# Retention and MLP interleaved on one core: one burst of small matmuls per chunk, and a reordered first batch

## The chip, the cores and the metric

The kernel runs on one core of a Trainium2 chip. The metric is the device time of one execution in microseconds (us), the median of several runs. Before the change it is 234.43 us (five runs, 233.9 to 240.18).

The engines are named as in the profile: PE is TensorE (the matrix array; PEld its weight loads), DVE is VectorE, ACT is ScalarE, POOL is GpSimd, SP is the sync engine, which here only issues DMAs. Each engine works through its own list of instructions in order.

## What is computed

Four batches, eight heads, 768 tokens, head size 64. A retention layer is followed by a low-rank token mixer and an MLP with a residual:

```python
for t in range(S):                       # per batch and head
    state = gamma * state + outer(k[t], v[t])
    y[t] = q[t] @ state / sqrt(D)
x = y, heads side by side                # [B, 768, 512]
h = x.transpose(0, 2, 1) @ U @ V         # low rank, over tokens; rank 32
u = x + h.transpose(0, 2, 1)
out = u + relu(u @ w_ch1) @ w_ch2        # 512 -> 2048 -> 512
```

Inputs and output are float32; the kernel computes its matmuls in bf16 and accumulates in float32 in PSUM.

## The kernel before

**Retention by chunks.** The recurrence is cut into chunks of 128 tokens, six per batch. For each chunk and head the kernel takes the *score* (k times q, masked to the causal half), the *mix* (masked score times v), the *query* (q times the state of the chunks before) and the *state* (k times v, added up in PSUM). The decay is put into q and v as factors when they are cast to bf16.

**Batches 1 to 3** are woven into the MLP of the batch before. `mlp_pieces` (L458) gives the MLP as a list of pieces with a cost: `up` pieces (L463: four matmuls and a relu, either 512 or 256 tokens wide, every third relu on DVE, the rest on ACT) and `down` pieces (L486: four matmuls; the last of a row adds the residual on DVE and queues a store). `weave` (L522) puts the pieces out in order and, at given fractions of their total cost (41.5 for a batch), calls the retention parts. The fractions are in `AT` and `LR` (L760 and L761), with one row for batch 1 and one for batches 2 and 3. For every chunk there are these calls:

- `turn_chunk` (L307): DVE turns k and q of the chunk, L313.
- `score4` (L356): sixteen matmuls on 32-row tiles of the array (L363), then two products with the mask on DVE (L369). In batches 2 and 3 the state follows at once (`state`, L332: sixteen matmuls on 32-column tiles, L348, and a copy on ACT to `ns`). In batch 1 k in natural order is first made with four matmuls (`natural_k`, L319).
- `mix4` (L377), a little later: sixteen query matmuls on 32-row tiles (L387; none for chunk 0), eight mix matmuls on the full array (L396), and two copies of x on ACT. In batch 1 the state comes behind it.
- `prep_chunk` (L266): POOL casts k, q and v of a later chunk (L83, L85). The order on POOL in batch 1 is k, q, v of chunk 0, then of chunk 1, and so on, with DMA issues for weights and for half of q between them.

Score and mix share the PSUM tiles `R[0]` and `R[1]`, two banks each. The tag `mlp` has three banks, used in turn by the MLP pieces and by `natural_k`. After the last chunk come `lr_proj` (L411), `lr_expand` (L421) and `lr_turn` (L436); in batches 2 and 3 the last is a DMA transpose issued by SP (L439).

**Batch 0** has no MLP to hide in and runs first, in 256-token blocks of its own layout, in an order written out by hand (L672 to L738): `cast_early`, `turn_early` (PE transposes and a copy), `score_early`, `state_early`, `query_early`, `mix_early`. At its end PE turns x (`x_turn`), forms the projection (`proj`, one copy `pc` on DVE), and adds the product with V (L732). The result is copied to `uT` in four pieces, two on ACT and two on DVE (L737). `late_consts` (L226) then makes the mask and the decay factors for the other batches: ten small DVE operations and two exponentials on ACT, and its second exponential needs the last of the DVE operations.

**DMA.** SP issues all input loads but those of the weights and part of batch 1's q, in program order with at most eight under way. Batch 1's v arrives by chunk at L133. POOL issues the weight loads (L291, L296), the rest of q and the stores (L456).

The order of each engine is the order of the program text as the weave calls it; tiles give the waits, and a PSUM bank that two engines use is handed from one to the other.

Of the kernel before, what the change touches and what calls it, by code (L numbers as in the profile page):

```python
# [10 lines left out]
bf16 = mybir.dt.bfloat16  # L11
# [5 lines left out]
def kernel(  # L17
# [12 lines left out]
    P = 128  # L30
# [39 lines left out]
    def evac(eng, dst, src):  # L70
        if eng == "A":
            nc.scalar.activation(dst, src, AF.Copy)  # L72
        else:
            nc.vector.tensor_copy(out=dst, in_=src)
# [241 lines left out]
    def turned(nm, b, ci, i, c, r=slice(None)):  # L316
        return bts[nm, b, ci][r, i, c]
# [12 lines left out]
        live["kn", b, ci] = kn  # L330

    def state(b, ci):  # L332
        if ci == NCK - 1:
            return
        vb = pre["v", b, ci]
        if b > 1:
            kd = pre.pop(("k", b, ci)).rearrange("p (n i) (c w) -> p i c n w",
                                                 i=2, c=2)
        else:
            kd = live.pop(("kn", b, ci))[:, :512].rearrange(  # L340
                "p (i c n w) -> p i c n w", i=2, c=2, n=4)
        if ci == 0:
            live["st_p", b] = bank("st")
        st_p = live["st_p", b]
        for i in range(2):
            for c in range(2):
                for hp in range(4):
                    nc.tensor.matmul(st_p[ds(32 * hp, 32), ts(2 * i + c, D)],  # L348
                                     kd[:, i, c, hp], vb[:, 2 * hp + i],
                                     start=(ci == 0 and i == 0 and c == 0),  # L350
                                     stop=True, skip_group_check=True)
        ns = rmid.tile([P, 320], bf16, tag="ns", name=f"ns_{b}_{ci}")
        evac("A", ns[:, :256], st_p[:, :256])
        live["state", b, ci] = ns

    def score4(b, ci):  # L356
        if b == 1:
            natural_k(b, ci)
        for i in range(2):
            for c in range(2):  # L360
                for hp in range(4):
                    r = ds(32 * hp, 32)
                    nc.tensor.matmul(R[hp // 2][:, hp % 2, ts(i, P)],  # L363
                                     turned("kT", b, ci, i, c, r),
                                     turned("qT", b, ci, i, c, r), start=(c == 0),
                                     stop=(c == 1))
        a = rmid.tile([P, H, P], bf16, tag="a4", name=f"a4_{b}_{ci}", bufs=3)
        for g in range(2):
            nc.vector.tensor_tensor(  # L369
                a[:, ds(4 * g, 4)].rearrange("p (n i) m -> p n i m", n=2),  # L370
                R[g][:, :, :256].rearrange("p n (i m) -> p n i m", i=2),
                mask[:, None, None, :].to_broadcast([P, 2, 2, P]), op=ALU.mult)
        live["a", b, ci] = a
        if b > 1:
            state(b, ci)

    def mix4(b, ci):  # L377
        if ci == 0 and b > 1:
            open_x(b)
        vb, a = pre["v", b, ci], live.pop(("a", b, ci))  # L380
        if ci:
            st = live.pop(("state", b, ci - 1))
            for i in range(2):
                for c in range(2):
                    for hp in range(4):
                        r = ds(32 * hp, 32)
                        nc.tensor.matmul(R[hp // 2][:, hp % 2, ts(i, D)],  # L387
                                         turned("qT", b, ci, i, c, r),
                                         st[r, ts(2 * i + c, D)],
                                         start=(i == 0 and c == 0), stop=False,  # L390
                                         skip_group_check=True)
        x4 = four(xs[b][:, ci])
        for g in range(2):
            for i in range(2):
                for hp in (2 * g, 2 * g + 1):
                    nc.tensor.matmul(R[g][:, hp % 2, ts(i, D)], a[:, 2 * hp + i],  # L396
                                     vb[:, 2 * hp + i],
                                     start=(ci == 0 and i == 0), stop=True,
                                     skip_group_check=True)
            evac("A", x4[:, ds(2 * g, 2)], R[g][:, :, :P])  # L400
        if b == 1:
            state(b, ci)
        pre.pop(("v", b, ci))

    us, uTs, pcs = {}, {}, {}

# [51 lines left out]
    def mlp_pieces(b):  # L458
# [17 lines left out]
            return f  # L476

        run = NM // 2 if b == 0 else NM
        for m0 in range(0, NM, run):
            for m in range(m0, m0 + run):  # L480
                pieces.append((0.864, up(m, 0, LO)))
            for m in range(m0, m0 + run):
                pieces.append((0.432, up(m, LO, S - LO)))
# [148 lines left out]
            if 2 * B0 + cc < LAST:  # L632
                query_early(2 * B0 + cc, o[cc])

    def mix_early(B0, engines="AA", open_mix=open_mix, late=None):
        if open_mix:
            open_mix(B0)
        o = mixing[B0]
        for g in range(2):
            a = eb["a", B0, g]  # L640
            for n in range(2):
                for i in range(2):
                    h = 4 * g + 2 * n + i
                    for j in range(2):
                        for cc in range(2):
                            r = ds(64 * cc, 64)
                            first = 2 * B0 + cc in (0, LAST) and h == 0 and j == 0
                            nc.tensor.matmul(
                                o[cc][:, ts(h, D)], a[r, 2 * i + n, ts(j, P)],
                                eb["v", B0][r, j, h], start=first, stop=True,  # L650
                                skip_group_check=True)
        if 2 * B0 + 1 == LAST:
            evac(engines[0], xs[0][:, 2 * B0], o[0])
            query_early(LAST, o[1])
            evac(engines[1], xs[0][:, LAST], o[1])
        else:
            evac(engines[0], xs[0][:, 2 * B0], o[0])
            if late:
                late(2 * B0 + 2)
            evac(engines[1], xs[0][:, 2 * B0 + 1], o[1])  # L660
        for key in (("a", B0, 0), ("a", B0, 1), ("qT", B0), ("v", B0), ("k", B0)):
            del eb[key]

# [18 lines left out]
    turn_early("k", 1)  # L682
    state_early(1)
    cast_early("q", 1, ("P", 4, 4), ("D", 0, 4))
    mix_early(0)
    turn_early("q", 1, "D")
    cast_early("v", 1, ("P", 0, 4), ("P", 4, 4))
    cast_early("q", 2, ("P", 4, 4), ("D", 0, 4))
    state_early(2)
# [3 lines left out]
    turn_early("q", 2)  # L693
    cast_early("k", 2, ("P", 0, 4), ("P", 4, 4))
    turn_early("k", 2, "D")
    cast_early("v", 2, ("P", 0, 4), ("P", 4, 4))
    load_uv()
    load_w1(1)
    cast_uv("u")
# [4 lines left out]
    cast_uv("v")  # L704
    open_mix(1)
    score_early(2)
    mix_early(1, "AD", open_mix=False, late=state_early)
    p_p = bank("mlp")

    def proj(js):  # L710
# [7 lines left out]
        for _ in range(n):  # L718
            nc.tensor.matmul(spare, ident, w1b[:, 0, :512], start=True, stop=True)

    mix_early(2, "DA")
    spare = bank("mlp")
    for c in range(NCB):
        x_turn(c, range(2))
    proj(range(4))
    for c in range(NCB):
        x_turn(c, range(2, 4))
    proj(range(4, NCK))
    pcs[0] = rmid.tile([P, P], bf16, tag="pc", name="pc_0")
    evac("D", pcs[0], p_p[:, :P])  # L730
    for c in (0, 2, 1, 3):
        nc.tensor.matmul(xT(c)[:, :LO], pcs[0][ds(RK * c, RK)],  # L732
                         V4[ds(RK * c, RK), :LO], start=False, stop=True,
                         skip_group_check=True)
    fill(2)
    for c in range(NCB):
        evac("AD"[c // 2], uTs[0][:, c, :LO], xT(c)[:, :LO])  # L737
    late_consts()  # L738
    n_cast[0] = 2 * NCK
    feed_more()  # L740
# [13 lines left out]
    for ci in range(3, NCK):  # L754
        prep_chunk(1, ci)

    def at(b0, dc, dm):
        return [(b0 + dc * ci, b0 + dc * ci + dm) for ci in range(NCK)]

    AT = {1: [(a, a + 0.042) for a in (0.19, 0.26, 0.33, 0.40, 0.465, 0.53)], 2: at(0.09, 0.105, 0.05)}  # L760
    LR = {1: (0.62, 0.66, 0.72, 0.78), 2: (0.69, 0.73, 0.80, 0.86)}  # L761
    def pause():
        hold_feed[0] = True

    for b in range(1, B):
# [4 lines left out]
        else:  # L770
            marks = [(0.03, part(lr_expand, 0, 4, 2)), (0.10, part(lr_turn, 0, 4)),
                     (0.16, part(lr_expand, 0, 0, 4))]
        step = AT[w][1][0] - AT[w][0][0]
        for ci in range(NCK):
            s_at, m_at = AT[w][ci]
            marks.append((s_at - 0.6 * step, part(turn_chunk, b, ci)))
            marks.append((s_at, part(score4, b, ci)))
            marks.append((m_at, part(mix4, b, ci)))
            if ci == NCK - 2:
                marks.append((s_at, pause))  # L780
            if b == 1:
                if ci < 3:
                    marks.append((0.86 + 0.05 * ci, part(prep_chunk, 2, ci)))
            elif ci + 3 < NCK:
                marks.append((s_at - 0.55 * step, part(prep_chunk, b, ci + 3)))
            elif b + 1 < B:
                marks.append((m_at + 0.05, part(prep_chunk, b + 1, ci - 3)))

        def mixed():
            lr_open(b)  # L790
# [42 lines left out]
```

## Time and profile before

| | us |
|---|---|
| median of five runs | 234.43 |
| lowest, highest | 233.9, 240.18 |
| the profiled execution | 238.09 |
| its span, first to last instruction | 236.3 |
| DVE, ACT, POOL busy in the span | 106.8, 79.0, 94.7 |
| TensorE clock granted, mean | 0.989 |

The profiled execution is one execution, and longer than the median; sums over its rows are to be read against its own 238.09 us. The stages of the span, with the time in which PE was busy:

| stage, us | what runs | PE busy, us |
|---|---|---|
| 0 to 28 | batch 0's retention | 18.25 |
| 28 to 88 | MLP of batch 0 with batch 1 woven in | 55.61 |
| 88 to 139.6 | MLP of batch 1 with batch 2 | 49.63 |
| 139.6 to 190 | MLP of batch 2 with batch 3 | 49.74 |
| 190 to 236.3 | MLP of batch 3, last stores | 41.43 |

A line of a timeline gives the start, the duration, the engine, the source line, the operation with its tiles and sizes, the count of merged instructions, and in brackets the idle time before it with what ended it. The start of a matmul is measured, its end is modelled, so gaps are best read from start to start. A few matmul records are missing in the trace (a row of x7 for eight matmuls).

### The profile page before, as it was taken

Reading aid. Unit: us, or ns where it says so; the run is one execution under the profiler, and the core shown is the slowest. Engines: PE = TensorE matmul, PEld = TensorE weight load, DVE = VectorE, ACT = ScalarE, POOL = GpSimd, SP = SyncE. Lnnn points to the kernel's source line nnn. Section 1 sums busy time; section 2 is a strip of 40 time slices with the busy share of each in tenths; the row PEclk is TensorE's granted clock in tenths of the full one; section 3 lists DMA queues with packets and bytes.
Section 4 is the critical chain, followed back from the end, with each engine's and each line's share of the span. In section 5 each row is a group of like instructions: output and inputs, shape, how many; then the busy total and the mean of one; then the engine's idle time right before and its main releaser. Section 6 shows DMA issues by size and latency. Waiting matters only on the chain.

```text
span 236.3 us, 5722 instructions
## 1 busy us (share of the span) xinstructions
PE 214.7 (91%) x2402; PEld 120.6 (51%) x2430; DVE 106.8 (45%) x200; ACT 79.0 (33%) x173; POOL 94.7 (40%) x132
## 2 busy tenths in 40 slices
PE   0589899995999999999999979999999999999992
PEld 0478545654644445457644434467444444674451
DVE  5367758553426226564444327546435142322121
ACT  2473465653511206555310015565310034540000
POOL 2797169774421189961059356600010100000110
PEclk9999999998899999999999999999999999999998
DMA  7999989999499999669999962000021620001212
GB/s 177 290 291 243 245 182 230 268 199 197 90 207 205 273 255 255 146 136 209 208 201 249 275 155 44 3 1 3 3 89 47 175 77 14 3 0 46 89 56 79
DMA packets 63882, 34.95 MB, mean 148 GB/s; under 512 B 40064, under 2 KB 61952, under 8 KB 63856
## 3 DMA queue, kind: packets, MB, share of 16 engines
q1 hardware_dynamic: 57344, 23.37, 47.6%
q0 software_dynamic: 6512, 11.21, 19.3%
q8 instruction: 19, 0.31, 0.6%
q14 instruction: 7, 0.06, 0.1%
HBM read 30.90 MB, written 6.29 MB: 157 GB/s over the span
## 4 chain that ended last, share of the span: by engine, by line
PE 53%; SPq 16%; DMA 15%; issue 8%; POOL 4%; DVE 2%; ACT 1%; POOLq 0%
PE mlp L467 27%; PE mlp L492 18%; SPq L149 9%; DMA v<-in_v_dram 8%; DMA kin<-in_k_dram 5%; SPq L176 3%; SPq L172 2%; SPq L439 2%; PE r L396 2%; DMA uT<-u 1%; PE r L363 1%; POOL out_dram L456 1%; POOL vb L85 1%; PE st L348 1%; PE r L387 1%
## 5 line engine op out<-in xcount | busy, mean ns | idle before, releaser
L467 PE MATMUL mlp<-uT,w1b 128*128 128x256 bf16 (+1 forms) x500 | 90.2, 327 | 2.8 <-DMA uT<-u 1.4
L492 PE MATMUL mlp<-w2b,gT 128*128 128x512 bf16 (+2 forms) x385 | 85.0, 371 | 1.0 <-issue 0.3
L474 ACT ACTIVATE gT<-mlp 128x512 bf16<-128x512 f32 (+1 forms) x88 | 42.7, 490 | 76.7 <-PE mlp L467 75.8
L467 PEld LDWEIGHTS <-w1b 128*128 128x128 bf16 x512 | 47.8, 98 | 33.6 <-issue 3.5
L492 PEld LDWEIGHTS <-gT 128*128 128x128 bf16 x400 | 37.1, 98 | 40.7 <-issue 0.2
L456 POOL DMA_DIRECT2D out_dram<-o x24 | 13.3, 555 | 92.8 <-DVE o L499 92.8
L499 DVE TENSOR_TENSOR o<-mlp,u 128x512 f32<-128x512 f32 (+2 forms) x25 | 16.7, 670 | 47.8 <-PE mlp L492 44.2
L472 DVE TENSOR_SCALAR gT<-mlp 128x512 bf16<-128x512 f32 (+1 forms) x40 | 22.0, 549 | 29.3 <-PE mlp L467 29.3
L369 DVE TENSOR_TENSOR a<-r,mask 128x512 bf16<-128x512 f32 x36 | 23.2, 685 | 16.8 <-PE r L363 12.3
L85 POOL TENSOR_TENSOR qi<-qin,gqT 128x512 bf16<-128x512 f32 x18 | 18.9, 1051 | 9.7 <-DMA qin<-in_q_dram 9.7
L72 ACT ACTIVATE x<-r 128x256 bf16<-128x256 f32 x36 | 11.8, 382 | 23.7 <-PE r L396 23.5
L83 POOL CAST ki<-kin 128x512 bf16<-128x512 f32 x18 | 13.8, 768 | 11.5 <-DMA kin<-in_k_dram 7.0
L431 DVE TENSOR_TENSOR u<-r,x 128x512 bf16<-128x512 f32 (+1 forms) x16 | 14.5, 950 | 4.1 <-PE r L424 3.5
L85 POOL TENSOR_TENSOR vd<-in,gk 128x512 bf16<-128x512 f32 x12 | 12.5, 1038 | 3.6 <-PE r L396 3.2
L313 DVE STREAM_TRANSPOSE kT<-ki 128x256 f32<-128x256 f32 x18 | 7.9, 438 | 5.3 <-POOL ki L83 5.1
L396 PE MATMUL r<-vd,a 128*128 128x64 bf16 x144 | 7.5, 197 | 2.4 <-POOL vd L85 2.4
L85 POOL TENSOR_TENSOR vd<-v,gk 128x512 bf16<-128x512 f32 x6 | 6.3, 1058 | 8.2 <-DMA v<-in_v_dram 5.0
L593 DVE TENSOR_TENSOR a<-r,mask 128x1024 bf16<-128x1024 f32 x6 | 7.1, 1219 | 4.6 <-PE r L588 3.2
L72 ACT ACTIVATE uT<-r 128x1024 bf16<-128x1024 f32 (+1 forms) x6 | 5.2, 880 | 11.4 <-PE r L445 9.7
L313 DVE STREAM_TRANSPOSE qT<-qi 128x256 f32<-128x256 f32 x18 | 7.4, 413 | 2.1 <-POOL qi L85 2.1
L363 PE MATMUL r<-qT,kT 32*128 32x128 bf16 x288 | 7.5, 217 | 1.0 <-DVE u L431 0.5
L566 PE MATMUL mlp<-ident,kb 128*128 128x128 bf16 x24 | 3.1, 312 | 5.5 <-DVE kb L83 5.5
(79 smaller groups left out, 140.7 us busy)
## 6 DMA issues: line engine op xcount, KB each, us to landing
out_dram<-o POOLq DMA_DIRECT2D x23, 256.0 KB, 3.2
v<-in_v_dram SPq DMA_DIRECT2D x12, 256.0 KB, 7.5
kin<-in_k_dram SPq DMA_DIRECT2D x8, 384.0 KB, 6.0
qin<-in_q_dram SPq DMA_DIRECT2D x8, 384.0 KB, 12.8
in<-in_k_dram SPq DMA_DIRECT2D x12, 256.0 KB, 5.8
in<-in_v_dram SPq DMA_DIRECT2D x12, 256.0 KB, 5.2
w1b<-in_moe_w_ch_dram POOLq DMA_DIRECT2D x4, 512.0 KB, 8.2
w2b<-in_moe_w_ch_dram POOLq DMA_DIRECT2D x4, 512.0 KB, 10.5
```

The costliest lines, as they stand in the source:

```text
L72: nc.scalar.activation(dst, src, AF.Copy)
L85: e.tensor_tensor(dst, src, scale, op=ALU.mult)
L149: nc.sync.dma_start(out=t.rearrange("p (h d) -> p h d", h=H), in_=src)
L313: nc.vector.transpose(out=dst, in_=src)
L369: nc.vector.tensor_tensor(a[:, ds(4 * g, 4)].rearrange("p (n i) m -> p n i m", n=2), R[g][:, :, :256].rearrange("p n (i m) -> p n i m", i= ...
L431: nc.vector.tensor_tensor(v4(us[b][:, ds(j0, nj), e]), R[g][:, :, :nj * P].rearrange("p c (j e) -> p c j e", j=nj), v4(xs[b][:, ds(j0, nj) ...
L456: nc.gpsimd.dma_start(out=dst, in_=src)
L467: nc.tensor.matmul(g_p[:, :sz], w1b[:, c, ts(m, P)], uTs[b][:, c, ds(lo, sz)], start=(c == 0), stop=(c == NCB - 1))
L472: nc.vector.tensor_relu(gT[:, m, ds(lo, sz)], g_p[:, :sz])
L474: nc.scalar.activation(gT[:, m, ds(lo, sz)], g_p[:, :sz], AF.Relu)
L492: nc.tensor.matmul(ch[:, :nn], gT[:, m, ts(j, P)], w2b[:, m, ds(n0, nn)], start=(m == 0), stop=(m == NM - 1))
L499: nc.vector.tensor_tensor(o_sb, ch[:, :nn], us[b][:, j, n], op=ALU.add)
```

## The change

Batches 1 to 3: `score4` and `mix4` are replaced by one function, `burst(b, n)`, which does the mix and query of chunk n, then the score of chunk n + 1, then the state of chunk n, without MLP pieces between them. The mix now goes first and the query adds to it, and both write to columns 256 to 383 of the R banks, beside the score in columns 0 to 255. The copies of x stand behind the mask products. A batch has seven bursts (n from -1 to 5; the first holds only a score, the last only a mix and query) where it had six scores and six mixes. The marks are moved accordingly.

Batch 0: block 1's q is turned by PE and copied by DVE ahead of the first mix; half of block 2's v is cast by DVE instead of POOL; part of the turning of x is done between the two halves of the last mix; `uT` is copied so that 256 tokens of all columns come first; and the first four rows of the MLP (m = 0 to 3) run as eight pieces 256 wide. One of two filling matmuls is left out.

```diff
+    def burst(b, n):
+        m = n + 1
+        mix, score = n >= 0, m < NCK
+        if score and b == 1:
+            natural_k(b, m)
+        if mix:
+            vb, a = pre["v", b, n], live.pop(("a", b, n))
+            (mix matmuls: R[g][:, hp % 2, ds(256 + D * i, D)], start=(i == 0))
+        if n > 0:
+            (query matmuls with state n - 1, into the same columns, start=False)
+        if score:
+            (score matmuls of chunk m: R[hp // 2][:, hp % 2, ts(i, P)])
+        if mix and score:
+            state(b, n)
+        for g in range(2):
+            if score:
+                nc.vector.tensor_tensor(a[...], R[g][:, :, :256], mask, op=ALU.mult)
+            if mix:
+                evac("A", four(xs[b][:, n])[:, ds(2 * g, 2)], R[g][:, :, ds(256, P)])
+        if mix and score:
+            evac("A", ns[:, :256], live["st_p", b][:, :256])
...
+        if b == 0:
+            for lo in (0, 256):
+                pieces += [(0.432, up(m, lo, 256)) for m in range(4)]
...
     cast_early("q", 1, ("P", 4, 4), ("D", 0, 4))
+    open_mix(0)
+    turn_early("q", 1, "D")
     mix_early(0)
-    turn_early("q", 1, "D")
...
-    cast_early("v", 2, ("P", 0, 4), ("P", 4, 4))
+    cast_early("v", 2, ("P", 0, 4), ("D", 4, 4))
...
-    mix_early(2, "DA")
+    open_mix(2)
+    mix_half(2, 0)
+    for c in range(2):
+        x_turn(c, range(3))
+    mix_half(2, 1)
...
-    fill(2)
-    for c in range(NCB):
-        evac("AD"[c // 2], uTs[0][:, c, :LO], xT(c)[:, :LO])
+    fill(1)
+    for lo in range(2):
+        for g in range(2):
+            evac("AD"[g], uTs[0][:, ds(2 * g, 2), ts(lo, 256)], R[g][:, :, ts(lo, 256)])
...
-    AT = {1: [(a, a + 0.042) for a in (0.19, 0.26, 0.33, 0.40, 0.465, 0.53)], 2: at(0.09, 0.105, 0.05)}
-    LR = {1: (0.62, 0.66, 0.72, 0.78), 2: (0.69, 0.73, 0.80, 0.86)}
+    AT = {1: (0.19, 0.26, 0.33, 0.40, 0.465, 0.53, 0.575),
+          2: [0.085 + 0.095 * i for i in range(NCK)] + [0.63]}
+    LR = {1: (0.62, 0.66, 0.72, 0.78), 2: (0.67, 0.71, 0.78, 0.84)}
...
-            marks.append((s_at, part(score4, b, ci)))
-            marks.append((m_at, part(mix4, b, ci)))
+            marks.append((at, part(burst, b, ci - 1)))
+            if ci == NCK - 1:
+                marks.append((nxt, part(burst, b, ci)))
```

The lines in brackets stand for loops of matmuls like those of `score4` and `mix4`. In the changed text of batch 0, `mix_half(B0, g)` is one half of the loop of `mix_early`, and `close_mix` frees its tiles. `AT` and `LR` of batches 2 and 3 move all calls to earlier fractions; in batch 1 the mix of chunk ci moves from `AT + 0.042` to the next chunk's mark.

## What the change is predicted to do

> **What bounds the kernel now.** I read the page's busy times, then the waits of TensorE (PE), then stages.
>
> ```profile
> PE 214.7 (91%) x2402; PEld 120.6 (51%) x2430; DVE 106.8 (45%) x200; ACT 79.0 (33%) x173; POOL 94.7 (40%) x132
> ...
> PE mlp L566 <- DVE kb L83: 5.5, 1, 5.5
> PE r L396 <- POOL vd L85: 2.4, 1, 2.4
> ...
> PE mlp L467 <- DMA uT<-u: 1.4, 1, 1.4
> ...
> PE r L363 <- DVE qT L313: 0.5, 1, 0.5
> ```
>
> PE is busy 91% of the span. Its idle time is the start and three waits: mix of batch 1's chunk 3 (2.4 us), its score of chunk 5 (0.5), and the first up matmul of batch 2's MLP (1.4), which waits for a DMA transpose. All three hang on DMA. The windows of busy time show what the first costs besides:
>
> ```profile
> 28.00:57.00 29.00, 26.04 (x338) 15.00 (x341) 18.43 (x40) 16.04 (x36) 19.20 (x26) 1.00 1.11 218
> 57.00:66.00 9.00, 7.78 (x127) 5.08 (x127) 3.71 (x8) 4.01 (x11) 5.75 (x7) 0.81 0.65 123
> ```
>
> The last three columns are granted clock, DMA share and GB/s: DMA is full until 57 us, and the clock is 0.81 right after the 2.4 us wait (half speed from 57.2 to 60.6, about 1.45 us lost). Batch 1's values come through GpSimd (POOL) in its timeline:
>
> ```profile
> 56.59 1.04 POOL L85 TENSOR_TENSOR vd<-v,gk 128x512 bf16<-128x512 f32 x1 [4.95 <-DMA v<-in_v_dram]
> 57.57 0.76 POOL L83 CAST ki<-kin 128x512 bf16<-128x512 f32 x1
> 58.26 1.05 POOL L85 TENSOR_TENSOR qi<-qin,gqT 128x512 bf16<-128x512 f32 x1
> 62.55 1.04 POOL L85 TENSOR_TENSOR vd<-v,gk 128x512 bf16<-128x512 f32 x1 [3.25 <-PE mlp L467]
> ```
>
> The second vd (chunk 4) is put down to PE, but its slot had long been free; I take it that v of chunk 4 landed at 62.4. From there vd, ki, qi and the DVE transpose take 3.4 us, and score of chunk 5 starts at 65.8. I call this moment S.
>
> Last, what one excursion from the MLP costs PE, in PE's timeline of batch 2 (start, us):
>
> ```profile
> 95.33 2.75 PE L467 MATMUL mlp<-uT,w1b 128*128 128x512 bf16 x12
> 98.01 0.40 PE L363 MATMUL r<-qT,kT 32*128 32x128 bf16 x16
> 98.35 0.30 PE L348 MATMUL st<-vd,kd 128*32 128x64 bf16 x16
> 98.58 1.90 PE L467 MATMUL mlp<-uT,w1b 128*128 128x512 bf16 x7
> 100.41 0.30 PE L387 MATMUL r<-ns,qT 32*128 32x64 bf16 x16
> 100.64 0.41 PE L396 MATMUL r<-vd,a 128*128 128x64 bf16 x8
> 100.88 2.75 PE L467 MATMUL mlp<-uT,w1b 128*128 128x512 bf16 x12
> ```
>
> Full-array matmuls start 216 ns apart (512 wide), so twelve from 95.33 end their turn at 97.92; L363 starts at 98.01. Read start to start, each change between full array, 32-row and 32-column tiles costs 88 to 105 ns (full to L363 311 instead of 216; L363 to L348 144 instead of 56; L348 to full 125 instead of 29, plus 11 at the next). L396 to full costs nothing.
>
> **What the Trainium skill says.** TensorEngine Tiling (Array Packing), Key Properties: a change of tiling mode drains the array. The trace agrees, at about 0.1 us. PSUM — Partial Sum Buffer, PSUM bank collisions raise a hardware error: the compiler orders any two engines on one bank, reads against reads too. Before has no such pair in these loops; the program after has it, since the copies of x now wait for DVE. TensorE: Matmul & The Clock Gate, What's actually happening: half clock after about one idle window of 3.4 us. The trace shows a half-speed stretch of 3.4 us after a 2.4 us wait.
>
> **The change part by part.**
>
> *Burst.* With the score as one change in and one out, batches 2 and 3 pay now: five scores with state 290 ns, one without 196, five mixes with query 200: 2.65 us. After: one score alone 196, five bursts (mix, query but in the first, score, state) 290, a last mix and query 200: 1.85. Gain 0.8 us each. Batch 1 (state behind the mix) goes from 3.17 to 1.85: 1.3 us. Matmul counts stay.
>
> Against it: the copy of x on ACT waits for the burst's end and for the mask product on DVE in the same bank; behind it on ACT stand ns and the relus of the next up pieces, for which PE waits with three mlp banks. Batch 3's stage shows the pattern already on DVE:
>
> ```profile
> 160.77 1.29 DVE L369 TENSOR_TENSOR a<-r,mask 128x512 bf16<-128x512 f32 x2 [0.85 <-ACT gT L474]
> 160.82 2.43 PE L467 MATMUL mlp<-uT,w1b 128*128 128x256 bf16 x18
> ...
> 161.97 0.42 DVE L472 TENSOR_SCALAR gT<-mlp 128x256 bf16<-128x256 f32 x1
> ```
>
> The relu on DVE sits behind the mask; the fourth 256-wide up after the score starts 405 ns after the third instead of 109 per matmul: 0.3 us lost. After, from the first mix matmul: score ends at 0.65, masks 0.97 to 2.26, copies of x to 2.70, ns to 2.98, first relu on ACT to 3.33. Three 512-wide ups (2.6 us) cover that; three 256-wide ones (1.3) don't. In batches 2 and 3 two bursts fall among 256-wide ups, both with a DVE relu first: 0.31+0.29 and 0.31, less the 0.30 paid now: +0.6 each. Bounds 0.3 (ACT's share overlaps better) to 0.6; I take 0.45. So batches 2 and 3 gain 0.35 each, 0.7 together. In batch 1 the bursts at 0.40 and 0.465 have an ACT relu first, up to 1.0 each; these two eat the 1.3.
>
> *Batch 1.* A burst needs the next chunk's k and q too. The burst with mix 3 therefore waits not for vd at 57.6 but for kT of chunk 4 (58.8) and its qT (59.8). POOL's order is unchanged and its work DMA-paced, so S stays at 65.8 and between 59.8 and 65.8 PE has about 4.2 us of work. After S before still owes 0.89 us of retention work, after 1.15 (state moved behind the score): +0.25. Without the DMA limit: -1.3+2.0 less the lead below, +0.2. I take +0.2.
>
> *Batch 0.* q turned ahead: PE transposes at 13.9 instead of 14.7, DVE copies q at 15.0 instead of 15.8; the chain score, mask, kT, score, mask runs 0.5 to 0.6 us earlier, mix of block 0 a microsecond later under DVE's cover. Half of v on DVE: 0.68 us between kT and a mask that waits for PE anyway (before idle 1.16 us there), POOL freed of 1.02. x turns before and behind the second half mix take about 0.5 us off: pc and the V product about 1.05 us earlier. 256-wide rows: the first up needs one copy per engine (0.65 us) rather than two (1.3): 0.35 earlier. But the first relu on ACT stands behind gqT, which waits for DVE's posT:
>
> ```profile
> 30.48 0.24 ACT L237 ACTIVATE gqT<-posT 128x48 f32<-128x48 f32 x1 [0.71 <-DVE posT L233]
> 30.63 1.06 ACT L474 ACTIVATE gT<-mlp 128x512 bf16<-128x512 f32 x2
> ```
>
> Three 256-wide ups last 1.3 us, not 2.6, so PE waits about 0.8 us for the first bank. Net lead 0.5 us. It comes before S, where PE has 2.4+0.5+1.45 of slack: worth 0 in the profiled run; if S came by PE, 0.5.
>
> *Marks.* Batch 2's projection comes 0.02 x 41.5 = 0.83 us earlier, so u and the DMA transposes could. But SP reached the first transpose only at 131.2, behind its loads, 0.8 after u: between 0 (SP bound) and -1.4 (wait gone). I take -0.35.
>
> **Sum.** +0.2 -0.7 -0.35 = -0.85 us. The profiled execution took 238.09 (span 236.3 and 1.8 around it), 3.7 above the median; taking away every wait and the half clock above gives 232.4, so the median run still holds about 2 us of such waits. On the median of 234.43: 233.6.
>
> **Rivals.**
> 1. Small gain as summed: 233.6, own range 232.9 to 234.2.
> 2. PE-bound in the usual run. The shorter median speaks for it, the full DMA until 57 against. The lead of 0.5, switches of 2.9 and the wait of 1.4 count, ACT's backlog only 1.5 to 2: about 231.8.
> 3. No net change: backlog at its upper bound (+0.25), transposes SP-bound (+0.35): 234.2.
> 4. Slower: the clock at the fourth burst of batch 1. PE idles there from about 55.4 to 58.8, 3.4 us instead of 2.6, then has only 1.4 us of work before the window from 57.2 to 60.6 ends, so half speed can last to 64.0. It decides if PE then reaches score 5 after qT is there; price 0.5 to 1.7 us. With +1.6 and the first sum: 235.2. For it the 0.81 above; against it the 1.7 us of slack before S.
>
> **Numbers.** Case 1 has 0.35 (0.22 of it beyond 0.3%), case 2 0.23, case 3 0.17, case 4 0.25. 0.3% of the median, 0.7 us, is about what can be told from no change. Faster 0.45, same 0.30, slower 0.25. Range 231.9 to 235.5.
>
> **What would show it.** Right: L387 and L396 matmuls next to L363 with no MLP between; PE idle before batch 1's fourth burst grown to about 3.4 us and ended by kT; S near 65.8 after the start; a PE wait on ACT or DVE of some 0.3 us after two bursts per batch; PE busy about 2 to 3 us less. Wrong: no idle there and S several us earlier (case 2), clock of the 57 to 66 stage under 0.7 (case 4), the transpose wait gone, or waits on ACT after 512-wide ups too.

## The result and the profile after

The kernel after is slower. Its median is 236.89 us (44 runs, 234.88 to 246.47), beside 235.12 for the kernel before (79 runs beside them, 232.5 to 241.9). The ratio is 1.0067 with a 95% interval of 1.005 to 1.0084, about 1.6 us, where 233.6 us, a ratio of 0.9965, had been forecast. Medians here count every execution and ratios leave disturbed ones out, so where the two seem to disagree the ratio is meant.

The first profile of after took 237.26 us (span 235.5). From its page: the clock that TensorE (PE) was granted in 40 slices, and the queue that brings PE its instructions (packets, MB, share).

```profile
PEclk9999999999999999999799999999999999999999
...
q8 instruction: 19, 0.31, 0.6%
```

The clock drops in one slice only, at about 113 us, in batch 2's stage. What PE waits for, in the view of waits of the kernel after (us in total, times, longest):

```profile
PE r L380 <- issue: 2.3, 1, 2.3
PE r L380 <- DVE u L433: 1.5, 2, 0.9
...
PE mlp L499 <- ACT gT L476: 0.8, 1, 0.8
PE mlp L469 <- ACT gT L476: 0.8, 1, 0.8
PE mlp L469 <- DVE gT L474: 0.8, 1, 0.8
```

The waits for `vd` and for the DMA transpose of `uT` are gone. The three of 0.8 us are in the forecast (L469 is `up`, L499 `down`). The two put down to ACT are ACT's copies behind DVE's masks in batch 1. The last is the fourth `up`: by the program it waits for an ACT relu behind `gqT`, and the view names a relu on DVE that ended 0.1 us earlier. The first two lines are not in the forecast. The second, at batch 1's first score, was 0.5 us in before; "Batch 0's two side effects" below comes back to it. In the first, "issue" means that nothing in the trace released PE: the score's matmuls (L380) had all their data and stopped. PE's timeline of the kernel after shows where:

```profile
109.70 0.29 PE L371 MATMUL r<-ns,qT 32*128 32x64 bf16 x16
109.83 0.38 PE L380 MATMUL r<-qT,kT 32*128 32x128 bf16 x13
112.47 0.23 PE L380 MATMUL r<-qT,kT 32*128 32x128 bf16 x3 [2.26 <-issue]
112.63 0.36 PE L346 MATMUL st<-vd,kd 128*32 128x64 bf16 x16
```

It stops behind the 13th of 16 score matmuls in the middle of one burst, then works at half speed from 112.73 to 116.15.

The first profile of before was an execution 3 us above the median. A second of each kernel (below) took 234.55 and 235.84 us, and is the fairer pair. The stages run from the first `up` of one batch to that of the next, and each is called after the batch whose retention is woven into it: batch 1's, batch 2's, batch 3's (bounds, length, then busy time of PE, PEld, DVE, ACT and POOL, granted clock, DMA share, GB/s). First of before, then of after, both from their second profile:

```profile
28.23:83.80 55.57, 54.15 (x636) 29.54 (x636) 28.61 (x58) 22.11 (x50) 32.16 (x42) 1.00 1.13 229
83.80:136.05 52.25, 50.49 (x585) 26.38 (x584) 25.55 (x46) 17.09 (x40) 29.23 (x40) 1.00 0.97 203
136.05:186.06 50.01, 49.87 (x577) 26.04 (x577) 24.18 (x44) 16.18 (x39) 12.60 (x17) 1.00 0.17 49
```

```profile
27.53:83.96 56.43, 52.61 (x653) 31.38 (x652) 29.43 (x60) 22.25 (x52) 32.12 (x42) 1.00 1.13 231
83.96:137.73 53.77, 51.51 (x586) 28.02 (x584) 24.70 (x45) 16.88 (x40) 28.73 (x38) 0.97 0.91 196
137.73:187.35 49.62, 49.32 (x577) 26.90 (x576) 24.70 (x45) 15.89 (x39) 13.14 (x18) 1.00 0.17 49
```

Batch 0 ends 0.70 us earlier, batch 1's stage is 0.86 longer, batch 2's 1.52 longer, batch 3's 0.39 shorter, the rest equal: +1.29, the difference of the spans. Everything but batch 2's stage sums to -0.23. In batch 2's stage the DMA share is 0.91 to 0.97; batch 3's, with the same work but a DMA share of 0.17, gains what it should.

### The profile page after: what moved, and what is told of

Same layout as the page of the kernel before. It is cut to its first block, busy times and chain, and to the rows that moved or that the text cites. A ratio compares the mean times of both kernels' runs of the same rounds, so it can differ in the third digit from the quotient of the medians.

```text
span 235.5 us, 5722 instructions
## 1 busy us (share of the span) xinstructions
PE 209.7 (89%) x2419; PEld 121.4 (52%) x2445; DVE 107.8 (46%) x203; ACT 78.8 (33%) x175; POOL 94.2 (40%) x131
## 4 chain that ended last, share of the span: by engine, by line
PE 38%; issue 33%; DMA 12%; SPq 8%; POOL 5%; DVE 2%; POOLq 0%; ACT 0%; DVEq 0%
PE mlp L499 17%; PE mlp L469 14%; DMA v<-in_v_dram 8%; DMA kin<-in_k_dram 3%; SPq L172 3%; SPq L176 3%; POOL out_dram L458 3%; SPq L124 2%; PE r L380 1%; DVE a L600 1%; PE r L361 1%; POOL vd L85 1%; POOL qi L85 1%; PE r L371 1%; PE st L346 1%
## 5 line engine op out<-in xcount | busy, mean ns | idle before, releaser
L469 PE MATMUL mlp<-uT,w1b 128*128 128x256 bf16 (+1 forms) x517 | 89.3, 323 | 2.8 <-ACT gT L476 0.8
L499 PE MATMUL mlp<-w2b,gT 128*128 128x512 bf16 (+2 forms) x385 | 84.9, 371 | 2.3 <-ACT gT L476 0.8
L469 PEld LDWEIGHTS <-w1b 128*128 128x128 bf16 x528 | 50.5, 99 | 34.0 <-issue 3.6
L476 ACT ACTIVATE gT<-mlp 128x256 bf16<-128x256 f32 (+1 forms) x90 | 41.7, 481 | 68.7 <-PE mlp L469 67.8
L499 PEld LDWEIGHTS <-gT 128*128 128x128 bf16 x400 | 37.6, 98 | 43.3 <-issue 2.1
L474 DVE TENSOR_SCALAR gT<-mlp 128x256 bf16<-128x256 f32 (+1 forms) x42 | 22.8, 542 | 25.4 <-PE mlp L469 25.4
L72 ACT ACTIVATE x<-r 128x256 bf16<-128x256 f32 x36 | 13.5, 384 | 33.7 <-DVE a L391 28.8
L380 PE MATMUL r<-qT,kT 32*128 32x128 bf16 x288 | 7.6, 215 | 3.8 <-issue 2.3
L83 POOL CAST kd<-in 128x512 bf16<-128x512 f32 x12 | 7.3, 610 | 6.0 <-issue 5.0
```

The costliest lines, as they stand in the source:

```text
L83: e.tensor_copy(out=dst, in_=src)
L469: nc.tensor.matmul(g_p[:, :sz], w1b[:, c, ts(m, P)], uTs[b][:, c, ds(lo, sz)], start=(c == 0), stop=(c == NCB - 1))
L474: nc.vector.tensor_relu(gT[:, m, ds(lo, sz)], g_p[:, :sz])
L476: nc.scalar.activation(gT[:, m, ds(lo, sz)], g_p[:, :sz], AF.Relu)
L499: nc.tensor.matmul(ch[:, :nn], gT[:, m, ts(j, P)], w2b[:, m, ds(n0, nn)], start=(m == 0), stop=(m == NM - 1))
```

## The experiments

Three theories stood at the start. A: PE runs out of fetched instructions in a burst. B: ACT's backlog behind the masks eats the saved switches. C: batch 0's part costs it.

**The two halves of the change, and the order of the copies.** `burst_only` keeps batch 0, `uT`'s copies and the first MLP rows of before; `b0_only` keeps `score4`, `mix4` and the marks of before. `x_first` turns the end of the burst round (arguments shortened):

```diff
         for g in range(2):
-            if score:
-                nc.vector.tensor_tensor(a[...], R[g][:, :, :256], mask, op=ALU.mult)
             if mix:
                 evac("A", four(xs[b][:, n])[:, ds(2 * g, 2)], R[g][:, :, ds(256, P)])
+        if score:
+            for g in range(2):
+                nc.vector.tensor_tensor(a[...], R[g][:, :, :256], mask, op=ALU.mult)
```

> The bursts and marks of the kernel after for batches 1 to 3, with batch 0 and the first MLP rows of the kernel before. Theory A (late instruction fetch in a burst): PE stops for one to three us inside some burst without a semaphore, perhaps at another burst since the program has fewer instructions ahead of it; ratio 1.000 to 1.010 with a stop, 0.991 to 0.997 without one. Theory B (ACT backlog): no such stop needed, ratio 1.004 to 1.009, PE waits for ACT or DVE gT of 2.5 to 4 us in sum. Theory C (batch 0): ratio 0.994 to 0.999.

Measured 1.0006 (0.9968 to 1.0043). PE does stop, in the same burst of batch 2 but 15 matmuls later, at the state (L346); even so the kernel is not measurably slower than before. From PE's timeline of `burst_only`:

```profile
107.77 0.27 PE L346 MATMUL st<-vd,kd 128*32 128x64 bf16 x12
110.22 0.21 PE L346 MATMUL st<-vd,kd 128*32 128x64 bf16 x4 [2.18 <-issue]
```

The program of `burst_only` has 30 PE instructions fewer ahead of this burst (4,879 instead of 4,909 in all; each matmul is two, a weight load and the product). Three score matmuls and twelve state matmuls are 15 matmuls, 30 instructions: counted from the start of the program, it is the same place.

> Batch 0 and the first MLP rows of the kernel after, with the separate scores and mixes and the marks of the kernel before for batches 1 to 3. Theory A and B: ratio 0.998 to 1.002, because the 0.9 us wait at the fourth up piece takes what batch 0 gains, and no stop of PE in batch 2. Theory C (batch 0 costs it): ratio 1.003 to 1.007, with the wait at the fourth up and a long wait for the first up in the trace.

Measured 0.9995 (0.9964 to 1.0026): no stop, a 2.1 us wait for `uT`, and the wait at the fourth `up`. By itself batch 0's part is worth nothing that can be told, so C alone is not the cause. Together with the bursts it does cost something, as the last part of this document shows.

> The kernel after with ACT's two copies of x emitted ahead of DVE's mask products in every burst, so that the copies wait for the burst and not for the masks, and the masks wait for the copies in the same bank. Theory B (ACT backlog): the stalls of 1.04 us after two bursts of batch 1 shrink to under 0.5, those of 0.4 in batches 2 and 3 change to waits for DVE relus of up to 0.4; time 0.5 to 1.5 us below the kernel after, ratio 1.000 to 1.005. Theory A (late fetch): the same gain of at most 1 us, but the stop of about 2.5 us at 110 us stays, since the program of PE is the same; ratio 1.003 to 1.007.

Measured 0.9951 (0.9911 to 0.999), below what either theory gave it. ACT's timeline in the same burst, first in the kernel after, then in `x_first`:

```profile
54.85 0.38 ACT L72 ACTIVATE x<-r 128x256 bf16<-128x256 f32 x1 [0.62 <-DVE a L391]
55.45 0.39 ACT L72 ACTIVATE x<-r 128x256 bf16<-128x256 f32 x1 [0.21 <-DVE a L391]
55.73 0.38 ACT L72 ACTIVATE ns<-st 128x256 bf16<-128x256 f32 x1
55.99 0.67 ACT L476 ACTIVATE gT<-mlp 128x256 bf16<-128x256 f32 x2
```

```profile
53.66 0.67 ACT L72 ACTIVATE x<-r 128x256 bf16<-128x256 f32 x2
54.19 0.42 ACT L72 ACTIVATE ns<-st 128x256 bf16<-128x256 f32 x1
54.45 0.43 ACT L477 ACTIVATE gT<-mlp 128x256 bf16<-128x256 f32 x1
```

In after the relu (L476) that frees PE's bank starts 2.0 us after the burst's state did (53.95), in `x_first` 1.0 us after it (53.49). Of PE's two gaps of 1.04 us in batch 1 one becomes 0.31 us and one vanishes; those of 0.40 us in batches 2 and 3 become 0.31, and the one of 0.31 us behind them is gone. (Two 256-wide matmuls start 0.11 us apart without a gap.) DVE's masks start some 0.4 us later, and PE does not wait for them. So the backlog of theory B has its part, 1.2% between the ratios of after and `x_first`; how much of that is the half-speed window, which did not follow in this profile, is not shown. The stop of PE at 107.7 us stayed, as theory A has it, at the same 13th matmul, 2.6 us long.

**Moving the packet boundary.** PE's instructions arrive in packets of 16,384 bytes. The Trainium skill (Runtime: NRT & Kernel Launch, Instruction fetch mechanics) gives 256 instructions to such a block, fetched by the sequencer through a DMA queue of its own, and calls the cost of crossing from one to the next mostly hidden. The trace agrees with the first: 19 packets on queue q8 for 4,909 instructions. To shift the boundary, tiny matmuls go into PE's idle time ahead of its first transpose, into a bank that is overwritten later: 64 in `fill64`, 8 in `fill8`.

```diff
+    for _ in range(64):
+        nc.tensor.matmul(R[0][:, 0, :8], ident, ident[:, :8], start=True, stop=True)
     cast_early("k", 0, ("D", 0, 4), ("D", 4, 4))
```

> The kernel after with 64 tiny matmuls (8 columns each, 128 PE instructions, into a bank that is overwritten later) put into PE's idle time before its first transpose; they add to the output nothing. They shift by 128 instructions the place at which PE's program is cut into the 256-instruction packets that its instruction queue fetches. Theory A (in the kernel after, PE runs out of fetched instructions in the burst behind chunk 3 of batch 2 and stops there 2.5 us, often with a half-speed window of the clock behind it): the stop at about 110 us is gone or stands elsewhere and is shorter, time 2 to 4 us below the kernel after, ratio to the kernel before 0.990 to 0.999. Theory B (the copies and relus of ACT behind the DVE masks eat the saved switches): the stop is chance, the time stays at 1.004 to 1.009. Theory C (batch 0 or the marks cost it): as B.

Measured 1.0087 (1.0051 to 1.0123). The stop is gone as A said, the time is not: PE waits 2.3 us for `uT` before batch 2's first `up`, with a half-speed window behind that. The forecast of A for the time was wrong: the stop had been hiding another wait.

> The kernel after with 8 tiny matmuls (16 PE instructions) in PE's idle time at the start. If the stop sits at a boundary of PE's 256-instruction packets: it stands 8 matmuls earlier in the same burst, behind the 5th matmul of the score instead of the 13th, about 2.5 us long, near 110 us. If the burst's own work or an unseen wait of the 14th score matmul causes it: it stays behind the 13th, or is gone. Time 235 to 238 either way.

Measured 234.97 us, in one execution. The stop did not move by 8 matmuls, it vanished, and in its place stands, in the view of waits of `fill8`:

```profile
PE mlp L469 <- DMA uT<-u: 1.6, 1, 1.6
```

The records of q8 say why the expectation missed. The packet in question began at 105.98 us in `fill8`, over 3 us ahead of the burst's first matmul (109.17); in after it began at 109.54, inside the burst (first matmul 109.37). A boundary 16 instructions earlier was enough for it to come in time.

| kernel | packet, us | PE stops behind | gap, start to start, us | PE goes on after the packet's end, us |
|---|---|---|---|---|
| after | 109.54 to 110.84 | score matmul 13 | 2.48 | 1.63 |
| after, second profile | 108.09 to 109.37 | 13 | 2.30 | 1.66 |
| `x_first` | 107.17 to 108.55 | 13 | 2.62 | 1.78 |
| `after_hold` (below) | 108.40 to 109.64 | 13 | 2.32 | 1.65 |
| `b0_mend` (below) | 107.86 to 109.17 | 13 | 2.27 | 1.59 |
| `burst_only` | 107.37 to 108.74 | state matmul 12 | 2.37 | 1.48 |

Six profiles, one place of the program, and a restart 1.5 to 1.8 us behind the packet each time ("13" is the 13th score matmul of the same burst).

**Taking the loads away.** `no_t3` leaves out 3.1 MB of loads that run from 98.8 us on (batch 3's k and q for the turned form; batch 3 works on batch 2's in their place), and leaves PE's program as it is.

```diff
+            if key[0] == "T" and key[1] == B - 1:
+                for nm in "kq":
+                    turned_in[nm, B - 1] = turned_in[nm, B - 2]
+                continue
```

> The kernel after without the loads of batch 3's turned k and q (3.1 MB, the L111 DMAs from 98.8 us on); batch 3 uses batch 2's k and q in their place, so its retention is computed from other data. PE's program is the same instruction for instruction. If PE's stop in the burst of batch 2 is a late instruction packet, late because the DMA engines are full with these loads: the stop at 110 us and the half-speed window behind it are gone, the uT transposes come some 10 us earlier in SP's list and PE doesn't wait for them; ratio 0.985 to 0.995. If the stop comes from PE's own work or from the program alone: it stays at the same matmul, and the ratio stays at 1.000 to 1.007.

PE runs through the burst. Its timeline in `no_t3` (L384 is the score, L350 the state):

```profile
117.38 0.39 PE L384 MATMUL r<-qT,kT 32*128 32x128 bf16 x16
117.70 0.30 PE L350 MATMUL st<-vd,kd 128*32 128x64 bf16 x16
```

The packet came at 112.61, over 4 us ahead of the burst, and batch 2's stage took 50.07 us with no wait for `uT`. Batch 1's inputs were late in this execution, so PE came to the burst 7.5 us later than in after (116.92 instead of 109.37), and the total is not used. The place in the program does not depend on that. Matched to the instructions of PE's program, the packet begins 63 to 75 instructions ahead of the one that waits for it in the six profiles of the table, 143 ahead in `no_t3`, and 200 to 303 ahead (at 256 to a packet) for all packets from 139 us on in these six, where the DMA share is below 0.3. So with the same PE program the packet comes late under the loads, as A has it.

**Taking the wait for uT away.** In SP's list batch 3's loads stand ahead of batch 2's `uT` transposes. These kernels load batch 3's k and v of chunks 3 to 5 behind the first transposes (`go` is set in `last_turn` of batch 2):

```diff
+            if key[0] in "kv" and key[1] == B - 1 and key[2] >= 3 and not go[0]:
+                return
             n_fed[0] += 1
```

> fill64 (the kernel after with the packet boundary moved by 64 matmuls, in which PE did not stop in the burst but waited 2.3 us for the uT transposes) with batch 3's k and v of chunks 3 to 5 loaded behind the uT transposes in SP's list rather than ahead of them. If the transposes are late because SP reaches them behind 30 us of loads: SP reaches them 6 to 7 us earlier or as soon as u is there, the wait of 2.3 us and the half-speed window behind it are gone, ratio 0.990 to 0.998 (fill64 had 1.0087). If the transposes are late because u is late: the wait stays and so does the ratio, 1.005 to 1.011.

The wait is gone and batch 2's stage took 50.07 us. No interval came out of its six runs (the profiled one, of 243.87 us, had lost its time in batch 1's stage, 66.78 us), so the question was put again as a pair:

> The kernel after with batch 3's k and v of chunks 3 to 5 loaded behind the uT transposes in SP's list; PE's program is that of the kernel after. If the stop is a late instruction packet at a fixed place of the program with the loads of 98 to 112 us around it (these are unchanged): the stop of about 2.4 us stays behind the 13th score matmul, no wait for uT; stage of batch 2 52.4 us, or 54 with a half-speed window behind it; ratio 1.002 to 1.008, as the kernel after. If the stop came from the later loads: it is gone, stage 50.1 us, ratio 0.990 to 0.997.

> after_hold with 8 tiny matmuls at the start, which move the packet boundary by 16 instructions. If the stop is a price of its own: no stop and no wait for uT, stage of batch 2 50.1 us, so 2.3 to 4 us below after_hold, ratio 0.988 to 0.997. If batch 2 is bound by something else: stage of 51.8 us or more with a new wait, ratio 1.000 to 1.006.

Measured 1.0055 (1.0011 to 1.01) for `after_hold` and 0.9964 (0.9942 to 0.9987) for `fill8_hold`. The two differ by eight tiny matmuls. Batch 2's stage in each, columns as above:

```profile
84.20:137.92 53.72, 50.83 (x579) 28.23 (x585) 24.75 (x45) 17.03 (x40) 28.77 (x38) 0.97 0.80 169
```

```profile
85.88:135.96 50.08, 49.19 (x578) 27.37 (x584) 24.70 (x45) 16.82 (x40) 28.16 (x37) 1.00 0.82 177
```

`after_hold` stops 2.3 us and runs one window at half speed (0.97 over the stage); `fill8_hold` does neither and is 3.64 us shorter there. In the ratios it is 0.9% or 2.1 us shorter; this execution of it came to the stage 1.68 us later (85.88 instead of 84.20), and the whole spans differ by 2.0 us (234.3 and 232.3). SP's timelines show what the later loads do, first in `fill8`, where the transposes stand behind all of them, then in `fill8_hold`:

```profile
125.94 1.99 SPq L149 DMA_DIRECT2D in<-in_v_dram  x1
128.03 13.93 SPq L441 DMA_TRANSPOSE uT<-u  x6
```

```profile
119.00 0.76 SPq L152 DMA_DIRECT2D in<-in_v_dram  x1
127.25 5.41 SPq L444 DMA_TRANSPOSE uT<-u  x4
132.70 0.58 SPq L152 DMA_DIRECT2D in<-in_k_dram  x1
```

In `fill8` SP is busy with loads until the moment it turns to `uT`; in `fill8_hold` it is free from about 120 us and waits for `u`.

> The kernel before with the same three chunks loaded behind the transposes. If the loads ahead of the transposes hold batch 2 there too: the wait for uT (1.4 and 1.6 us in two profiles) is gone, stage of batch 2 50.4 instead of 52.0 to 52.3, ratio 0.990 to 0.996. If the wait depends on u and not on the loads: the wait stays, ratio 0.998 to 1.002.

Measured 0.9952 (0.9921 to 0.9984), batch 2's stage 50.63 us, no wait for `uT`. The profiled execution, of 239.07 us, had lost its time in batch 1's stage (61.23 us); in batch 2's its clock was full. The kernel before was held by the same loads.

**Second profiles.**

> The kernel after once more, for a second profile. If the stop belongs to the program (the place of its packet boundary and the loads around it): PE stops again behind the 13th score matmul of the burst after chunk 3 of batch 2, 2.3 to 2.7 us, or, if the packet just came in time, it waits 1 to 2.5 us for uT instead. If it was chance: neither, and the stage of batch 2 takes about 50.1 us.

> The kernel before once more, for a second profile, since the first was 3 us above the median. If batch 2 is bound by the loads and the DMA transposes behind them: a wait for uT of 1.5 us or more again, or its stage of 51.5 to 53 us. The 2.6 us wait for v of chunk 3 in batch 1 and the half-speed window behind it are gone or shorter in a run near the median.

Both came out by their first case: the stop again (2.3 us, half-speed window from 112.1), and in before the wait for `uT` again (1.6 us), with 0.7 us left of the wait for `vd`. They are the pair of the first section.

**Batch 0's two side effects.** `b0_mend` calls `late_consts()` ahead of `proj(range(4))`, and keeps the count for "every third relu" from being shifted by the four extra pieces:

```diff
                 n[0] += 1
+                if b == 0 and n[0] == 9:
+                    n[0] = 5
```

> The kernel after with two mends at batch 0's end: the decay constants (ten DVE operations, two exponentials) are made ahead of the projection, while DVE waits for pc, and the count that gives every third relu to DVE skips the four extra pieces, so that DVE has the same later relus as in the kernel before. Theory: these two cost the kernel after 0.9 us at the fourth up piece and 1.1 us at the first score of batch 1. Both waits gone (the score's back to under 0.8 us), MLP of batch 0 about 2 us shorter (54.5 to 55.2 instead of 56.7); of that the total keeps between 0 (if the loads bound batch 2, and the wait for uT grows by 2) and 2: ratio 0.998 to 1.006.

Measured 1.0028 (0.9998 to 1.0058), batch 1's stage 55.09 us. The wait at the fourth `up` (gap of 0.97 us) is gone. The two gaps at batch 1's first score went only from 0.81 and 1.13 us to 0.37 and 1.13, so the count explains the first of them and not the second. The second gap of 1.04 us in batch 1 is down to 0.41. And `pc`, now behind the constants on DVE, comes 0.64 us later after the last projection matmul. The stop of PE stayed.

**Putting it together.**

> x_first (0.9951), with the 64 tiny matmuls of fill64 and the later loads of fill64_hold: no stop in the burst of batch 2, no wait for uT, no ACT backlog. If the three losses are separate: the span of x_first's profile (231.7) less 2.5 for the stop, less 1.6 where a half-speed window followed it, so about 229 in the profile and a ratio of 0.975 to 0.986. If they only trade places (batch 2 is bound by the loads of batch 3 in another way): ratio 0.990 to 0.997, with a new wait of PE in 100 to 140 us.

Measured 0.993 (0.9892 to 0.9967); the profile has no stop, no wait for `uT` and full clock throughout, with stages of 54.89, 49.73 and 49.30 us. The three losses are gone, yet the ratio is not the 0.975 to 0.986 that was expected for that case. Batch 0 ends at 29.74 us here and at 27.71 in `x_first`; what delays it is not shown, and the tiny matmuls may not be free.

> best1 with the two mends of b0_mend. Nothing of PE's waits is left to hide the gain in batch 2, so if batch 1's inputs come in time the whole 2 us shows: span of an undisturbed run about 228.5, ratio 0.984 to 0.990. If batch 1 is bound by its own inputs (v and kT landing at 52 to 60 us): ratio 0.990 to 0.995, with longer waits at 50 to 62 us.

Measured 0.9967 (0.9937 to 0.9997), outside both expectations: the mends add nothing that can be told on top of `best1`.

> burst_only (batch 0 and first MLP rows of the kernel before) with the copies of x ahead of the masks, the later loads, and 79 tiny matmuls at the start, which put the packet boundaries where best1 has them. If batch 0's part of the change costs what the stages say (some 1.5 us in the MLP of batch 0 for 0 to 0.7 us of lead): MLP of batch 0 53.2 to 54 us, batches 2 and 3 49.7 and 49.3, span of an undisturbed run 228 to 229.5, ratio 0.980 to 0.990. If batch 0's part is worth its lead: ratio 0.991 to 0.998.

Measured 0.9914 (0.9874 to 0.9954). There is only the time, no profile, and its interval overlaps that of `best1`: whether batch 0's old form is the better one here as well stays open. Both beat the kernel before and the kernel after.

## Why the prediction was wrong

**The step that failed** is batch 2's share of the sum: -0.35 us for its bursts and -0.35 for the marks. Measured on the pair of second profiles it is +1.52, off by 2.2 of the 2.4 us that lie between forecast (-0.85) and ratio (+1.6). The forecast knew only semaphores as a cause for PE to wait. It missed that a burst puts 56 matmuls, 112 instructions, into about 1.0 us (from 116.92 to 117.94 in `no_t3`), while an `up` or `down` takes 0.43 to 0.86 us for eight. With the DMA engines full of batch 3's loads (a share of 1.11 to 1.15 between 100 and 112 us in after, 0.30 in the 4.4 us ahead of the burst in `no_t3`) the next packet comes too late for that. The stop costs 2.3 to 2.6 us, and a half-speed window behind it about 1.3 more (stages of 53.7 to 53.9 us with it, 52.3 and 52.5 without, in `b0_mend` and `x_first`).

**The wait for uT** did disappear, as the lower bound of the marks had it, but only because PE arrives later. Where the stop is moved away it is back (1.6 and 2.3 us). So the term was chosen between the right bounds, and what it stands for is a floor: with the loads ahead of the transposes, batch 2's stage takes 51.9 to 53.0 us whatever PE saves in it (`fill8` 51.85, before 51.98 and 52.25, `fill64` 52.55, `b0_only` 52.95).

**The bursts' own price** was right. With neither stop nor wait the stage is 50.08 us in `fill8_hold` and 50.63 in `before_hold`; batch 3's is 49.62 instead of 50.01. That is 0.55 and 0.39 for a forecast of 0.35. The backlog on ACT was sized right as well (gaps of 0.31 to 0.40 us in batches 2 and 3, 1.04 twice in batch 1), and `x_first` shows that it is a matter of order, not of the burst.

**Batch 0 and batch 1.** The wait of 0.8 us at the fourth `up` came as forecast. The lead of 1.05 us for the V product did not: it ends 0.70 us earlier in the second pair of profiles and not at all in the first. Together with the 0.86 us longer stage of batch 1, which holds that wait, the two parts sum to +0.16; the forecast had +0.2. That they agree is luck. `burst_only`, with the batch 0 of before, comes to the end of batch 1's stage at 82.85 us, where before's second profile has 83.80 and after's 83.96: there the bursts gain about 1 us in batch 1 instead of losing 0.2, and batch 0's part, put at nothing, takes 1.1 us back (the waits at the fourth `up` and at batch 1's first score, and one of the two gaps of 1.04 us, of which `burst_only` has one). The ratios say the same. PE stops in `burst_only` as it does in after, and the ratio is 1.0006 (0.9968 to 1.0043) instead of 1.0067 (1.005 to 1.0084). Score of chunk 5 was not pinned at 65.8 us: it starts at 61.3 in the second profile of before and at 63.2 in the first of after, with v there in time, so the idle of 3.4 us ahead of the fourth burst did not come either.

**The rivals.** The fourth, half speed after a longer idle time, had a part of the mechanism, the slow clock, and nearly the right time (235.2), at the wrong place and without the stop: not at batch 1's fourth burst behind a DMA, but in batch 2 behind an instruction packet. The measured time is 235.12 times 1.0067, 236.7, or 236.0 on the median that the forecast was made against, in both cases outside the range.

Without the stop and with the later loads, the change (`fill8_hold`, 0.9964) and the kernel before (`before_hold`, 0.9952) cannot be told apart: as it stands, the change is worth about nothing. It lost against before because its stop, with the slow clock behind it (0.9% between `after_hold` and `fill8_hold`), costs more than before's wait for `uT` (0.5% in `before_hold`). The stop alone does not make a slower kernel: `burst_only`, without batch 0's part, and `x_first`, without the backlog on ACT (0.9951), stop as well and are not measurably slower than before.

## What to carry to other kernels

When small matmuls are packed together, count instructions and not only their time: a stretch that uses up a large part of an instruction packet within a microsecond (here 112 of 256) can outrun its fetch while the DMA engines are full, and the trace then shows "issue" with nothing to wait for. Before crediting a saving to a stage, ask what else ends it; here the loads ahead of a transpose in SP's list put a floor under batch 2 that swallowed the gain there. And copies that free a bank for a later engine belong ahead of products that nobody waits for yet.

## What the hardware showed beyond expectation

Crossing from one instruction packet to the next is not always hidden: it cost 2.3 to 2.6 us in six profiles, and 16 instructions more ahead of it made it vanish. Against the "mostly hidden" of the Trainium skill (Runtime: NRT & Kernel Launch, Instruction fetch mechanics) the measurement decides. The traces show when a packet starts and ends, not when it is asked for; how the loads delay it stays open.

Eleven profiles have a gap of 2.3 to 2.7 us in PE's work. In nine a half-speed window followed: at the stop in after, its second profile, `after_hold` and `burst_only`, at the wait for `uT` in `fill64` and `b0_only`, and in batch 1's stage in before, `fill64_hold` and `best2`. It lasted 3.4 us, in `best2` 6.8. None followed in `x_first` (2.62 us) and `b0_mend` (2.27 us), nor behind gaps of 2.0 us (`fill8`, second profile of before). The Trainium skill's idle window of 3.4 us (TensorE: Matmul & The Clock Gate, What's actually happening) has the right length for the slow stretch, but the gap that brings it on can be shorter.
